# Half-array matmul pairs in two pieces ordered through GpSimd, with new load queues and a new planned order, in a kernel of sliding-window attention and a state-space layer

## The chip, the cores and the metric

The kernel runs on one core of a Trainium2 chip. The metric is the device time of one execution in microseconds (us); lower is better.

## The reference

Two independent layers read inputs of 2048 tokens by 448 features, in bf16, and their results stand side by side in the output (2048 x 896).

```python
# A: attention over 8 keys, 2 tokens apart, 16 heads of 28
qkv = x @ wqkv
logits = einsum("bhsd,bhswd->bhsw", q, k[s - 2*w, w = 0..7]) * 28**-0.5   # masked where s - 2w < 0
a = (softmax(logits) @ v) @ wo
# B: diagonal complex state-space layer with 448 states
Lam_bar = exp(dt * Lam);  B_bar = ((Lam_bar - 1) / Lam)[:, None] * Bmat
h[t] = Lam_bar * h[t-1] + B_bar @ x[t]
y = 2 * real(h @ Cmat.T) + x * Dskip
out = concatenate([a, y], axis=-1)
```

## The kernel before

**Layout.** Two tokens are taken together, so there are 1024 rows of 896 features, which lie across partitions as seven tiles of 128 (`xA`, `xB`, loaded by transposing DMAs). The even token's 448 features are tiles 0 to 2 and the lower half of tile 3, the odd token's the upper half of tile 3 and tiles 4 to 6. A product of both tokens with one weight matrix is therefore made of matmuls with 64 partitions: the lower and the upper half of the TensorE array work side by side, one for each token, and at the fifth pair they change places, so that each writes into the PSUM bank the other wrote into before. That is `pairs` (line 491): four pairs, a `PE.drain()`, three pairs. The weights must lie in both halves of the partitions, so copies on DVE fill the second one: `n_vw` (459) for V, `n_wp` (464) and `n_wo2` (471) for Q and K, which are also padded from 28 to 32 columns a head.

**Work units.** The kernel builds a list of nodes, each with its engine or engines, a cost, dependencies and a rank:

- `v0` to `v8` (596): V for nine blocks of 128 rows, evicted by `ev`; `q{q}{s}{c}` (611): Q (q = 0) and K (q = 1) for four groups of heads s and two chunks c of 512 rows, evicted by `eq`.
- `s{par}{b}` (647): scores of one token of the pair for block b; `x` (648, 649): their exponentials on ACT; `a{b}` (666): probabilities times V; `n{b}` (667): the normalisation on DVE (a reciprocal at 663 and a product at 664); `ot{b}`: a transposing DMA of the result.
- `l1`, `l2`, `wtx` (561 to 563): the state-space input weights, made from parameters and tables (`tr`, `pA` to `p3`, `t0` to `t4`) and transposed by DMA; `b{hf}{k}` (749): input products for half hf of the rows and state tile k (k = 3 is half as big), evicted by `be`.
- For each `b`: `ma`, `ri`, `sc`, `mb`, `ro` on DVE (704 to 748): a rotation, the scan, the rotation back, giving the states h. The scans of half 1 start from the end of half 0.
- `cg`, `ch` (779, 780): output weights C from the transposed C, on ACT and DVE; `g0`, `g1`: products C x B for the odd tokens.
- `y{t}` (845): output of the state-space layer for 128 rows; it needs every `ro` of its half, all C and both g. `w{t}` (861): the attention output projection, by `pairs`. Each is evicted to `ys` and stored from SP.

**Order.** `Plan.run` (64) walks through the nodes with a clock for each engine and always takes the ready node of the lowest rank. Its result is the order in which instructions are written; at run time each engine works strictly in that order and waits where an operand isn't there. Four PSUM units of two banks (pool `mm`) are shared by all products; scores take two at once. Nodes that free a unit get a rank below all others (`node`, 510). `RANK` (27) is an empty table. Outside the plan, ahead of it, stand the loads (281 to 296) and GpSimd's constants (301 to 336: identity, zeros of the padding, masks, ones, and four loads of `Ctn`).

```python
for part in (range(4), range(4, 7)):
    for z, (ps, n, lhs, rhs) in enumerate(jobs):
        if part[0]:
            PE.drain()
        for i in part:
            a, b = (0, 1) if i < 4 else (1, 0)
            x = PE.matmul(ps[:, a, 0:n], lhs(0, lo[i]), rhs(0, lo[i]), ...)
            y = PE.matmul(ps[:, b, 0:n], lhs(64, hi[i]), rhs(64, hi[i]), ...)
```

A last part (from line 894) branches into an exact attention when a sum of exponentials overflowed; it isn't taken with these inputs.

Of the kernel before, what the change touches and what calls it, by code (L numbers as in the profile page):

```python
# [17 lines left out]
HALF = 512  # L18
# [8 lines left out]
RANK = {}  # L27
# [185 lines left out]
def kernel(  # L213
# [66 lines left out]
    xbar_x(xA, xA2, 0, 128)  # L280
    ACT.dma_start(Wv[:, 0:3, :], A_wqkv[0:384, 2 * D:3 * D].rearrange("(k p) n -> p k n", p=128))
    ACT.dma_start(Wv[0:64, 3, :], A_wqkv[384:448, 2 * D:3 * D])
    xbar_x(xA, xA2, 128, 256)
    ACT.dma_start(Wraw[:, 0:3, :], A_wqkv[0:384, 0:2 * D].rearrange("(k p) n -> p k n", p=128))
    ACT.dma_start(Wraw[0:64, 3, :], A_wqkv[384:448, 0:2 * D])
    for i, vec in enumerate((B_Lambda_re, B_Lambda_im, B_log_dt, B_Dskip)):
        G.dma_start(rows[7 * i:7 * i + 7, :], vec.rearrange("(c p) -> c p", p=64))
# [22 lines left out]
    G.memset(m0, 1.0)  # L310
    sel(v16(m1), v16(m0), [[0, 8], [1, 16]], ALU.is_equal, 0.0, 0, -1)
    sel(v8(m2), v8(m0), [[1, 16], [0, 8]], ALU.is_equal, 0.0, 16, -1)
    G.tensor_tensor(msk[0:32, 0, :], m1, m2, ALU.add)
    G.memset(m0, 0.0)
    sel(v16(m1), v16(m0), [[0, 8], [-1, 16]], ALU.is_ge, NEG, 7, 1)
    sel(v16(m2), v16(m0), [[0, 8], [1, 16]], ALU.is_ge, NEG, 0, -1)
    sel(v16(m2), v16(m2), [[0, 8], [1, 16]], ALU.is_ge, 0.0, 8, -1)
    G.tensor_tensor(m1, m1, m2, ALU.add)
    sel(m1, m1, [[0, 128]], ALU.is_ge, 0.0, 15, -1)
    sel(m2, m0, [[1, 128]], ALU.is_ge, NEG, 128, -8)  # L320
    sel(m2, m2, [[-1, 128]], ALU.is_ge, NEG, -114, 8)
    sel(m2, m2, [[0, 128]], ALU.is_ge, 0.0, -16, 1)
    G.tensor_tensor(msk[0:32, 1, :], m1, m2, ALU.add)
    for g in range(1, 4):
        G.tensor_copy(msk[32 * g:32 * g + 32, :, :], msk[0:32, :, :])
    G.memset(Vt[:, :, :, :, 28:29].rearrange("p a b h o -> p (a b h) o"), 1.0)
    for i in range(3):
        G.memset(Pb[i][:, :, :, 112:128], 0.0)
    G.memset(rcs[:], 1.0)
    G.memset(Gm[64:128, 3, :], 0.0)  # L330
    ct_r = B_C_re[:, 384:448].rearrange("(k p) n -> p k n", p=112)
    ct_i = B_C_im[:, 384:448].rearrange("(k p) n -> p k n", p=112)
    G.dma_start(Ctn[:, :, 0:64], ct_r)
    G.dma_start(Ctn[:, :, 64:128], ct_i)
    G.dma_start(Ctn[:, :, 128:192], ct_i)
    G.dma_start(Ctn[:, :, 192:256], ct_r)

    def diag():
        dgE = lazy["dgE"] = t_([128, 4, 128], BF16, "dgE", "rG")
        for k in range(4):  # L340
# [21 lines left out]
    lre, lim, ld = f32[:, 0], f32[:, 1], f32[:, 2]  # L362
# [125 lines left out]
    turn = tc.alloc_semaphore("turn")  # L488
    turns = [0]

    def pairs(jobs):

        lo, hi = (0, 1, 2, 3, 4, 5, 6), (4, 5, 6, 3, 0, 1, 2)
        last = {}
        for part in (range(4), range(4, 7)):
            for z, (ps, n, lhs, rhs) in enumerate(jobs):
                if part[0]:
                    PE.drain()  # L500
# [427 lines left out]
```

## Time and profile before

| | |
|---|---|
| median of 3 runs | 169.62 us (169.33 to 170.07) |
| the profiled execution | 167.73 us |
| its span, first to last instruction | 166.0 us |
| busy in the span: PE / DVE / ACT / GpSimd | 142.3 / 100.1 / 92.6 / 18.9 us |
| mean granted clock of TensorE | 0.925 |

PE is TensorE, whose weight loads (PEld) run beside its matmuls; DVE is VectorE, ACT ScalarE, POOL GpSimd, SP the engine that issues most of the DMAs. A busy PE counts matmuls that lie over each other once; the granted clock is 1.0 at 2.4 GHz and 0.5 at 1.2 GHz. In the chain of waits every piece of time is given to what released the next step, back from the last instruction.

### The profile page before, as it was taken

The numbers are of one execution on the slowest core, as the hardware profiler recorded it, in microseconds if no ns is written. First come the engines' busy times: TensorE is split into PE (matmuls) and PEld (weight loads), VectorE is DVE, ScalarE is ACT, GpSimd is POOL, SyncE is SP. The second block draws the span as 40 slices with busy tenths as digits, with TensorE's granted clock in tenths as the row PEclk, the third lists the DMA queues.
The fourth block names the chain that finished last, engine by engine and source line by source line (L and its number), as shares of the span: only waits on it lengthen the run. The fifth ranks groups of instructions, "written<-read, shape, count | busy, mean of one in ns | idle before, by whom it ended". The sixth has DMA issues, their size and how long they took to land.

```text
span 166.0 us, 3493 instructions
## 1 busy us (share of the span) xinstructions
PE 142.3 (86%) x1424; PEld 66.2 (40%) x1430; DVE 100.1 (60%) x210; ACT 92.6 (56%) x113; POOL 18.9 (11%) x48
## 2 busy tenths in 40 slices
PE   6839799999999999999999865963999999999950
PEld 2213234333344434345455453740353443345530
DVE  0545599679999997989999999999300000000000
ACT  2023897884559896679777497980025325523320
POOL 7989900000000000000000000000000000000000
PEclk9987999999999999999999995555599999999998
DMA  5999998338981020200202020622531331513111
GB/s 128 217 231 228 230 213 153 69 70 155 191 158 32 0 57 4 48 4 0 52 0 48 6 48 18 82 52 48 132 116 55 115 111 56 170 60 111 55 59 61
DMA packets 39924, 15.13 MB, mean 91 GB/s; under 512 B 32928, under 2 KB 39840, under 8 KB 39904
## 3 DMA queue, kind: packets, MB, share of 16 engines
q1 hardware_dynamic: 38688, 13.42, 36.2%
q10 hardware_dynamic: 960, 1.20, 3.2%
q0 software_dynamic: 256, 0.23, 0.7%
q8 instruction: 13, 0.21, 0.5%
q14 instruction: 7, 0.06, 0.1%
HBM read 3.16 MB, written 3.67 MB: 41 GB/s over the span
## 4 chain that ended last, share of the span: by engine, by line
PE 60%; DVE 23%; DMA 5%; issue 4%; ACT 4%; SPq 1%; ACTq 0%; DVEq 0%
PE mm L503 29%; PE mm L697 8%; PE mm L837 7%; PE mm L833 6%; DMA xA<-in_A_x_dram 5%; PE mm L835 4%; DVE O L664 4%; DVE C L774 3%; DVE rs L731 3%; PE mm L657 2%; PE mm L504 2%; DVE ra L710 2%; DVE rb L711 1%; DVE rcs L663 1%; ACT P L645 1%
## 5 line engine op out<-in xcount | busy, mean ns | idle before, releaser
L478 ACT CAST ys<-mm 128x896 bf16<-128x896 f32 x16 | 14.5, 905 | 35.4 <-PE mm L840 29.3
L645 ACT ACTIVATE P<-mm 128x896 bf16<-128x896 f32 (+1 forms) x36 | 31.2, 936 | 2.3 <-PE mm L639 2.3
L503 PE MATMUL mm<-xA,Wpad 64*128 64x512 bf16 x112 | 28.7, 378 | 1.3
L504 PE MATMUL mm<-xA,Wpad 64*128 64x512 bf16 x112 | 28.6, 378 | 1.0 <-DVE Wpad L474 1.0
L697 PE MATMUL mm<-xB,WT 128*128 128x512 bf16 x92 | 22.2, 380 | 0.7 <-ACT u L478 0.3
L503 PE MATMUL mm<-Wv,xA 64*128 64x448 bf16 x63 | 16.0, 378 | 3.7 <-DMA xA<-in_A_x_dram 3.0
L504 PE MATMUL mm<-Wv,xA 64*128 64x448 bf16 x63 | 15.9, 378 | 0.4 <-DVE Wv L462 0.4
L833 PE MATMUL mm<-C,h 128*128 128x448 bf16 x56 | 13.5, 379 | 2.9 <-DVE C L774 2.9
L503 PEld LDWEIGHTS <-Wpad 64*128 64x128 bf16 x112 | 8.7, 94 | 17.5 <-issue 10.0
L697 PEld LDWEIGHTS <-WT 128*128 128x128 bf16 x98 | 9.1, 97 | 11.4 <-issue 1.1
L478 ACT CAST Vt<-mm 128x896 bf16<-128x896 f32 x8 | 7.3, 906 | 11.2 <-PE mm L504 11.0
L503 PE MATMUL mm<-wo,OT 64*128 64x448 bf16 x56 | 12.8, 351 | 0.7
L837 PE MATMUL mm<-C,h 128*128 128x448 bf16 x56 | 13.0, 376 | 0.0
L884 DVE TENSOR_SCALAR flag<-mm 1x1 int32<-1x1 f32 x1 | 0.1, 146 | 21.3 <-PE mm L881 21.3
L504 PE MATMUL mm<-wo,OT 64*128 64x448 bf16 x56 | 12.8, 351 | 0.0
L635 PE MATMUL mm<-msk 32*128 32x448 bf16 (+1 forms) x72 | 9.6, 401 | 3.3 <-DVE O L664 3.1
L657 PE MATMUL mm<-Vt,P 128*128 128x29 bf16 x288 | 9.4, 180 | 2.3 <-ACT P L645 2.3
L503 PEld LDWEIGHTS <-xA 64*128 64x128 bf16 x63 | 5.2, 97 | 13.5 <-issue 6.4
L657 PEld LDWEIGHTS <-P 128*128 128x128 bf16 x288 | 8.5, 99 | 4.5 <-issue 2.1
L664 DVE TENSOR_TENSOR O<-mm,rcs 112x896 bf16<-112x896 f32 (+1 forms) x9 | 9.8, 1092 | 0.3
L478 ACT CAST Kt<-mm 128x1024 bf16<-128x1024 f32 x7 | 7.1, 1012 | 4.6 <-PE mm L504 4.6
L504 PEld LDWEIGHTS <-Wpad 64*128 64x128 bf16 x112 | 8.7, 94 | 1.7 <-DVE Wpad L474 1.5
(171 smaller groups left out, 232.8 us busy)
## 6 DMA issues: line engine op xcount, KB each, us to landing
out_dram<-ys SPq DMA_DIRECT2D x16, 224.0 KB, 2.4
Wraw<-in_A_wqkv_dram ACTq DMA_DIRECT2D x1, 672.0 KB, 7.5
wo<-in_A_wo_dram SPq DMA_DIRECT2D x2, 336.0 KB, 3.4
Wv<-in_A_wqkv_dram ACTq DMA_DIRECT2D x1, 336.0 KB, 3.3
natW<-in_B_B_re_dram SPq DMA_DIRECT2D x1, 336.0 KB, 3.7
natW<-in_B_B_im_dram SPq DMA_DIRECT2D x1, 336.0 KB, 4.5
OT<-O SPq DMA_TRANSPOSE x9, 2.5
Wraw<-in_A_wqkv_dram ACTq DMA_DIRECT2D x1, 112.0 KB, 8.4
```

The costliest lines, as they stand in the source:

```text
L478: ACT.copy(o, i)
L503: x = PE.matmul(ps[:, a, 0:n], lhs(0, lo[i]), rhs(0, lo[i]), start=(i == 0), stop=(i == 6), skip_group_check=True)
L504: y = PE.matmul(ps[:, b, 0:n], lhs(64, hi[i]), rhs(64, hi[i]), start=(i == 0), stop=(i == 6), skip_group_check=True)
L635: PE.matmul(at(g)[:, 0:4 * n].rearrange("p (s q) -> p s q", s=4), msk[32 * g:32 * g + 32, 0, :], msk[32 * g:32 * g + 32, 1:2, c0:c0 + n].t ...
L645: ACT.activation(P[:].rearrange("p s g q -> p g s q")[:, 2 * z:2 * z + 2, :, 0:n], h["s"][z][:, :, 0:4 * n].rearrange("p g (s q) -> p g s ...
L657: PE.matmul(av[:, par, 29 * hd:29 * hd + 29], hb_[par]["P"][:, hd // 4, hd % 4, :], Vt[:, par, b, hd, :], start=True, stop=True)
L664: V.tensor_tensor(O[0:n, :].rearrange("p (a h d) -> p a h d", a=2, h=H), avv[0:n, :, :, 0:DH], rc.unsqueeze(3).to_broadcast((n, 2, H, DH)) ...
L697: PE.matmul(ps[:, i, :], WT[:, j, 128 * m:128 * m + 128], xB[:, j, HALF * hf:HALF * hf + HALF], start=(j == 0), stop=(j == 6))
L731: V.tensor_tensor_scan(h["s"][:, i], p["r2"][:, k:k + 1].to_broadcast((128, HALF)), h["v"][:, i], 0.0 if hf == 0 else ini[:, m:m + 1], ALU ...
L833: PE.matmul(ps[:, 0, 0:D], hb[:, m, lo:lo + 128], lazy["C2"][:, m, :], start=(m == 0), stop=False, skip_group_check=True)
L835: PE.matmul(ps[:, 0, 0:D], xB[:, k, tk], Gm[:, k, :], start=False, stop=(k == 3), skip_group_check=True)
L837: PE.matmul(ps[:, 1, 0:D], hb[:, m, lo + 1:lo + 129], lazy["C1"][:, m, :], start=(m == 0), stop=False, skip_group_check=True)
```

## The change

1. `pairs` becomes `pair`, called twice for a block: first with four pairs, later with three. Between them a node on GpSimd (`relay`) writes one element of `tick` after the last two matmuls of the first piece, and the first matmul of the second piece waits for that write. `PE.drain()` is gone. The planner (`halves`) puts the pieces and the relays into the order like other nodes, the relay with a rank below almost everything.
2. Q and K are made for 256, 256 and 512 rows instead of 512 and 512, which is 24 blocks instead of 16, each waiting for its half of the padded weights. `n_wp` does one half of the columns with all copies into the other partitions (`n_wo2` is gone), and may go to ACT or DVE.
3. Loads: the four parameter rows move from GpSimd's queue to ACT's, in another order; Wraw moves from ACT's to SP's, between the first and the second piece of `xA`.
4. GpSimd's constants, the `Ctn` loads and the two diagonals become nodes of the plan, which other nodes depend on; the planner's GpSimd clock starts at 1.3 instead of 16.0.
5. The ranks are a line each in `RANK` (a base and a step for each kind of node), replacing numbers in the code; DVE's part of the scans (`d0`, `d1`) and their products (`b0`, `b1`) have ranks of their own, and `s` and `a` count down in part, so attention blocks come in the order 1, 0, 8, 7, ... 2. Some costs and arrival times of the planner are other numbers.

```diff
-RANK = {}
+RANK = {"v": (-66.54, 10.223), "q0": (48.53, -16.849), "q1": (28.45, 7.586), "s": (-0.92, -1.464), "a": (-18.79, 2.805), ...}
...
     xbar_x(xA, xA2, 0, 128)
-    ACT.dma_start(Wraw[:, 0:3, :], ...)
-    for i, vec in enumerate((B_Lambda_re, B_Lambda_im, B_log_dt, B_Dskip)):
-        G.dma_start(rows[7 * i:7 * i + 7, :], ...)
+    SP.dma_start(Wraw[:, 0:3, :], ...)
     xbar_x(xA, xA2, 128, 256)
...
-    def n_wp(e, q):
+    def n_wp(e, q, z):
+        o = Wpad[:, :, q, 256 * z:256 * z + 256].rearrange(...)[:, :, :, 0:DH]
...
         f(o[0:64, 3], i[0:64, 3])
+        f(o[64:128, 3], i[0:64, 0])
+        f(o[0:64, 4:7], i[64:128, 0:3])
+        f(o[64:128, 4:7], i[0:64, 1:4])
...
-    def pairs(jobs):
+    def behind(x, y):
+        tc.add_manual_dep(x.ins, y.ins.name, SYNC, reason="row tiles")
+    def pair(h, part, ps, n, lhs, rhs):
...
+        for i in (range(4), range(4, 7))[part]:
+            a, b = (0, 1) if i < 4 else (1, 0)
+            x = PE.matmul(ps[:, a, 0:n], lhs(0, lo[i]), rhs(0, lo[i]), ...)
+            y = PE.matmul(ps[:, b, 0:n], lhs(64, hi[i]), rhs(64, hi[i]), ...)
+            if i == 4:
+                behind(x, h["tick"])
+        if part == 0:
+            h["done"] = (x, y)
+
+    def relay(h):
+        k = h["tick"] = G.memset(tick[:, 0:1], 0.0)
+        behind(k, h["done"][0])
+        behind(k, h["done"][1])
...
+    def halves(name, cost, fn, deps, rank, h, at):
+        x = node(name + "_", {"P": 4 * cost}, lambda e: fn(0), deps, rank, alloc="mm", at=at, mode="h")
+        k = node(name + "k", {"G": 0.12}, lambda e: relay(h), [x], -200)
+        return x, node(name, {"P": 3 * cost}, lambda e: fn(1), [k], -50, mode="h")
...
-    for c in range(2):
+    CH = ((0, 256), (256, 512), (512, 1024))
+    for c, (t0_, t1_) in enumerate(CH):
...
-        n1 = node(f"w{t}", {"P": 1.33}, pe, need + [wl], 62 + 3 * t, alloc="mm", mode="h")
+        n0, n1 = halves(f"w{t}", 0.188, pe, need + [wl], ("w", t), h, 0.0)
...
-    plan.run({"P": 5.6, "A": 4.4, "V": 1.0, "S": 19.0, "G": 16.0})
+    plan.run({"P": 5.7, "A": 4.4, "V": 1.0, "S": 19.5, "G": 1.3})
```

On GpSimd, among its constants at the start, before (`mst` and `msk` are the masks, `Vt` gets its column of ones):

```order
L300 AFFINE_SELECT mst<-mst 32x128 x3
L318 TENSOR_TENSOR mst<-mst 32x128
L300 AFFINE_SELECT mst<-mst 32x128 x4
L323 TENSOR_TENSOR msk<-mst 32x128
L325 COPY msk<-msk 32x256 x3
L326 MEMSET Vt 128x288
L328 MEMSET P_79 128x16x16
```

and now, with a relay's memset of `tick` among them:

```order
L536 MEMSET tick 1x1
L333 TENSOR_TENSOR mst<-mst 32x128
L303 AFFINE_SELECT mst<-mst 32x128 x4
L340 TENSOR_TENSOR msk<-mst 32x128
L536 MEMSET tick 1x1
L344 COPY msk<-msk 32x256 x3
L536 MEMSET tick 1x1
L347 MEMSET Vt 128x288
L536 MEMSET tick 1x1
L351 MEMSET P_79 128x16x16
```

The constants stand in the same sequence; the relays of the first four half-array blocks (two of V, two of K and Q) have come to stand between them.

On ACT, from the late exponentials (`P`) to the output evictions (`ys`), before:

```order
L645 ACTIVATE P_81<-mm 128x2x4x112 x2
L645 ACTIVATE P_79<-mm 128x2x4x112 x2
L645 ACTIVATE P_80<-mm 128x2x4x112 x2
L484 ACTIVATE wtmp<-CT,p_ph 128x448
L645 ACTIVATE P_81<-mm 128x2x4x112 x2
L484 ACTIVATE wtmp<-CT,p_ph 128x448
L478 CAST ys<-mm 128x896 x16
```

and now:

```order
L505 CAST u<-mm 128x512
L698 ACTIVATE P_81<-mm 128x2x4x112 x2
L505 CAST ys<-mm 128x896
L698 ACTIVATE P_80<-mm 128x2x4x112 x2
L505 CAST ys<-mm 128x896
L698 ACTIVATE P_79<-mm 128x2x4x112 x2
L505 CAST ys<-mm 128x896
```

All sixteen output evictions stood behind the last exponential; now nine stand ahead of it, five behind, and two are on DVE. The products `y0` to `y6` and `w` stand on PE between the scores in the same way: y0, scores, y1, scores, attention, y2, scores, y3, scores, attention, w0, w5, scores, w6, w7, attention, scores, y4, scores, y5, attention, y6, w3, w4, w1, w2, y7.

On DVE, from the last scan (`rs`) to the guard (`one`), before (`h` are the states, `C` the output weights, `O` the normalised attention):

```order
L731 SCALAR_TENSOR_TENSOR rs<-p_r_160,ini,rv 128x512
L663 RECIPROCAL rcs<-mm 112x32
L664 TENSOR_TENSOR O<-mm,rcs 112x896
L713 TENSOR_TENSOR ra<-rs,tab 128x512
L714 TENSOR_TENSOR ra<-rs,tab 128x512
L744 TENSOR_TENSOR h_1268<-ra 64x512
L745 TENSOR_TENSOR h_1268<-ra 64x512
L774 SCALAR_TENSOR_TENSOR C_1483<-CT,p_sh,wtmp 128x448 x2
L873 MEMSET one 128x1
```

and now:

```order
L784 SCALAR_TENSOR_TENSOR rs<-p_r_120,ini,rv 128x512
L766 TENSOR_TENSOR ra<-rs,tab 128x512
L767 TENSOR_TENSOR ra<-rs,tab 128x512
L797 TENSOR_TENSOR h_1711<-ra 64x512
L798 TENSOR_TENSOR h_1711<-ra 64x512
L716 RECIPROCAL rcs<-mm 112x32
L717 TENSOR_TENSOR O<-mm,rcs 112x896
L716 RECIPROCAL rcs<-mm 112x32
L717 TENSOR_TENSOR O<-mm,rcs 112x896
L927 MEMSET one 128x1
```

The two C instructions behind the last states have moved ahead of the second half's scans, and two normalisations now come behind the last states.

## Rows read from the trace of the kernel before

**Rows 1.** The page's second part: granted TensorE clock, in tenths, 40 slices of 4.15 us.

```profile
PEclk9987999999999999999999995555599999999998
```

**Rows 2.** Stage windows: stretch, length, busy us (count) of PE PEld DVE ACT POOL, clock, DMA.

```profile
4.10:41.80 37.70, 31.96 (x240) 11.67 (x241) 26.78 (x84) 22.70 (x30) 15.98 (x39) 0.95 0.88 175
41.80:90.00 48.20, 46.56 (x556) 21.71 (x558) 45.67 (x80) 37.05 (x44) 0.00 (x0) 1.00 0.25 49
90.00:115.30 25.30, 17.58 (x343) 11.52 (x342) 24.72 (x41) 17.32 (x23) 0.00 (x0) 0.70 0.22 38
115.30:160.30 45.00, 43.40 (x284) 20.29 (x283) 2.57 (x7) 13.61 (x16) 0.00 (x0) 0.94 0.31 98
```

**Rows 3.** The chain that ended last, in order of time: start, us, what.

```profile
55.30 0.90 PE mm L657 x32
...
80.29 3.13 PE mm L697 x14
...
84.22 0.30 PE mm L635 x4
84.52 0.25 PE mm L639 x16
...
108.30 1.09 DVE O L664
...
115.31 1.28 DVE C L774 x2
116.64 0.53 PE mm L833
...
152.99 1.32 PE mm L833 x7
...
156.59 1.32 PE mm L833 x7
...
160.27 0.91 ACT ys L478
```

**Rows 4.** Timeline of PE, QK and w blocks, lower half of the array: start, us, instruction.

```profile
29.50 0.38 PE L503 MATMUL mm<-xA,Wpad 64*128 64x512 bf16 x1
...
29.97 0.38 PE L503 MATMUL mm<-xA,Wpad 64*128 64x512 bf16 x1
...
140.92 0.35 PE L503 MATMUL mm<-wo,OT 64*128 64x448 bf16 x1
...
141.11 0.35 PE L503 MATMUL mm<-wo,OT 64*128 64x448 bf16 x1
...
141.55 0.36 PE L503 MATMUL mm<-wo,OT 64*128 64x448 bf16 x1
```

**Rows 5.** Timeline of the first 19 us, all engines; in brackets idle time and what ended it.

```profile
0.31 0.10 POOL L912 MEMSET const-float32-0.0<- 128x1 f32 x1 [0.31 <-issue]
...
4.11 1.21 DVE L460 COPY Wv<-Wv 64x448 bf16<-64x448 bf16 x1 [2.84 <-DMA Wv<-in_A_wqkv_dram]
...
9.43 0.63 DVE L468 COPY Wpad<-Wraw 128x1344 bf16<-128x1344 bf16 x1 [3.03 <-DMA Wraw<-in_A_wqkv_dram]
...
10.95 0.36 PE L503 MATMUL mm<-Wv,xA 64*128 64x448 bf16 x1 [2.76 <-DMA xA<-in_A_x_dram]
...
17.98 1.04 POOL L336 DMA_DIRECT2D Ctn<-in_B_C_re_dram  x1
```

**Rows 6.** Groups by line on DVE: count, busy us, mean ns, idle before.

```profile
L480 DVE CAST u<-mm 128x1024 bf16<-128x1024 f32 (+1 forms) x2 | 1.9, 954 | 0.8 <-PE mm L697 0.8
...
L480 DVE CAST Kt<-mm 128x1024 bf16<-128x1024 f32 x1 | 1.2, 1218 | 0.0
...
L480 DVE CAST Vt<-mm 128x896 bf16<-128x896 f32 x1 | 1.1, 1095 | 1.5 <-PE mm L504 1.5
...
L473 DVE COPY Wpad<-Wpad 64x3072 bf16<-64x3072 bf16 x1 | 1.0, 1015 | 0.0
...
L469 DVE COPY Wpad<-Wraw 64x448 bf16<-64x448 bf16 x2 | 0.7, 351 | 0.9 <-DMA Wraw<-in_A_wqkv_dram 0.9
```

More of the change, by code (lines that the diff above doesn't have):

```diff
@@ L309 @@
     v8 = lambda m: m.rearrange("p (a b) -> p a b", b=8)
[L310 to L328, printed above, removed]
@@ L329, with g_eye, g_iota, g_pad @@
-    G.memset(rcs[:], 1.0)
-    G.memset(Gm[64:128, 3, :], 0.0)
+    def g_eye(e):
+        G.memset(eye[:], 1.0)
+        sel(eye[:], eye[:], [[1, 128]], ALU.is_equal, 0.0, 0, -1)
+    def g_iota(e):
+        G.iota(iota, [[1, HALF]], base=1, channel_multiplier=0, allow_small_or_imprecise_dtypes=True)
+    def g_pad(e):
+        G.memset(Wpad[:, :, :, :].rearrange("p k q (h c) -> p (k q h) c", c=32)[:, :, 28:32], 0.0)
+    def g_m1(e):
+        G.memset(m0, 1.0)
+        sel(v16(m1), v16(m0), [[0, 8], [1, 16]], ALU.is_equal, 0.0, 0, -1)
+        sel(v8(m2), v8(m0), [[1, 16], [0, 8]], ALU.is_equal, 0.0, 16, -1)
+        G.tensor_tensor(msk[0:32, 0, :], m1, m2, ALU.add)
@@ L331, with g_m5, g_one, g_zero @@
+    def g_m5(e):
+        for g in range(1, 4):
+            G.tensor_copy(msk[32 * g:32 * g + 32, :, :], msk[0:32, :, :])
+    def g_one(e):
+        G.memset(Vt[:, :, :, :, 28:29].rearrange("p a b h o -> p (a b h) o"), 1.0)
+    def g_zero(e):
+        for i in range(3):
+            G.memset(Pb[i][:, :, :, 112:128], 0.0)
+        G.memset(Gm[64:128, 3, :], 0.0)
+    def g_rcs(e):
+        G.memset(rcs[:], 1.0)
     ct_r = B_C_re[:, 384:448].rearrange("(k p) n -> p k n", p=112)
     ct_i = B_C_im[:, 384:448].rearrange("(k p) n -> p k n", p=112)
-    G.dma_start(Ctn[:, :, 0:64], ct_r)
@@ L784 @@
     gn = []
-    dg = [n for n in plan.nodes if n["name"] == "dia"]
+    dg = [n for n in plan.nodes if n["name"] in ("dgE", "dgO")]
     for z in range(2):
@@ L850, with pe @@
         h = {}
-        def pe(e, tk=tk, h=h):
-            ps = h["ps"] = unit()
+        def pe(part, tk=tk, h=h):
+            if part == 0:
+                h["ps"] = unit()
             o, w = OT(), lazy["wo"]
-            pairs([(ps, D, lambda o_, k: o[o_:o_ + 64, k, tk], lambda o_, k: w[o_:o_ + 64, k, :])])
+            pair(h, part, h["ps"], D, lambda o_, k: o[o_:o_ + 64, k, tk], lambda o_, k: w[o_:o_ + 64, k, :])
         def ev(e, h=h):
```

205 lines of the change are left out of this document (111 added, 94 removed).

## Prediction

> **What bounds the kernel now.** Read the page's slices of the granted clock first: it is full nearly everywhere, but stands at 8 and 7 tenths in slices 3 and 4 and at 5 in slices 25 to 29, where PE was waiting [rows 1]. The stage windows say who is the limit there. From 41.8 to 90 PE and DVE are both full (46.6 and 45.7 of 48.2 us). From 90 to 115.3 DVE has 24.7 of 25.3 us, PE only 17.6, at a mean clock of 0.70. After 115.3 DVE is as good as done (2.6 of 45.0 us) and PE works alone, 43.4 of 45.0 us [rows 2]. The chain shows why the two don't overlap: the last scan's result and the last two C instructions on DVE end at 116.6, and only then can the first output matmul finish; all eight y blocks and all eight w blocks stand behind that, to 160.2, with an eviction and a store of 5.8 us after it [rows 3]. So the tail of 45 us is PE work, part of which could have run while PE waited for DVE.
>
> **The half-array pairs.** A w block starts a pair of matmuls every 0.19 us, but 0.44 us pass from its fourth pair to its fifth (141.11 to 141.55); a QK block, takes 0.215 a pair for its 512 columns (0.19 x 512 / 448), and 0.47 there (29.50 to 29.97) [rows 4]. A drain thus costs 0.25 to 0.26 us, and 9 v, 16 QK and 8 w blocks have one each: 33 x 0.25 = 8.4 us of PE time. After the change a relay on GpSimd stands there (41 of them, as 8 QK blocks are split in two), and the order puts at least three pairs of another block between. The relay is not in this trace. Its parts: a memset of one column 0.10 us [rows 5], a handover like DVE's to PE, 0.05 us (115.31 + 1.28 to 116.64) [rows 3], twice; and the last pair ends 0.16 us after its slot (0.35 long, 0.19 apart [rows 4]). That makes 0.36 us from the end of the slot, against a cover of three pairs, 0.57 us (448 columns), 0.64 (512) or 0.32 to 0.43 (256). So I take 0 for it. Lower bound 0; upper bound the drain's 0.25 us each, if GpSimd takes three times as long as its row.
>
> **QK in 256-token pieces.** The columns are the same: 16 half blocks of 0.75 us for 8 of 1.50. Each matmul now has half the columns, with as many weight loads. The attention rows run 32 matmuls of 29 columns, each with a full weight load, in 0.90 us [rows 3], 28 ns each, far below the 107 ns of a 256-column pair; I take nothing, and at most 0.08 us (the loads as long as a 448-column pair) x 7 pairs for the 5 pieces behind the start of the scans, 2.8 us.
>
> **PE's work in the new order.** Units from rows: b 3.13 (14 matmuls), scores 0.30 + 0.25, attention 0.90, y 3.60 (152.99 to 156.59) [rows 3]; v and w 7 x 0.19 = 1.33, QK 7 x 0.215 = 1.50 [rows 4]; the two g together 4 x 1.32 + 0.3 = 5.6. Before the scans: v 11.2 (less the piece done at 6 us), QK 11 x 0.75 + 4 x 1.50 = 14.3, one small b 1.57, one score 0.55: 27.6 us. From there to y4: six b and a small one 20.4, 16 scores 8.8, 8 attentions 7.2, QK 9.8, g 5.6, **four y 14.4 and four w 5.3**: 71.4. From y4 on: 14.4 + 0.55 + 0.9 + 5.3 = 21.2. In all 120.2 us. Switches between half-array, quarter and full-array work are 47 in both orders, so they change nothing.
>
> **The loads.** PE waited for the second piece of x until 10.95 and DVE for Wraw until 9.43, while the three x pieces and Wraw ran from two queues [rows 5]. Now Wraw stands between the first and second piece of x on SP, and the third piece behind both. I take 10.0 for the second piece (bounds 9 and 12, the latter if Wraw's issue of 1.1 us only pushes it back). The parameter rows move from GpSimd to ACT, which lets GpSimd start its constants earlier. Against this, the four Ctn issues (about 1 us each [rows 5]) now stand between two relays; the cover there is about 2.65 us of PE work, so some 1.2 us show, and some 0.3 at another constant. The lost clock of slices 3 and 4, 0.5 x 4.15 = 2.1 us [rows 1], I leave in, as PE still waits before that load. PE reaches the first big b at 10.0 + 27.6 + 3.9 = 41.5.
>
> **DVE.** Up to the first scan it was busy 26.8 of 37.7 us [rows 2]. Evictions: before 1.22 + 1.10 + 1.22, after five of 1.10, six of 0.69 (1.9 for two, less 1.22) and one of 1.22 [rows 6], +7.3; the Wpad copies go from 10752 columns to 4928, at 1.015 us for 3072 [rows 6], -1.9, the other two nodes being on ACT, which has 15 us free there [rows 2]. That is 32.2. Of 10.9 us idle, 3.0 alone was the wait for Wraw [rows 5], which comes sooner, as do the parameter rows; I keep 4.0 (bounds 2 and 10.9). First scan at 4.1 + 32.2 + 4.0 = 40.3, against 41.8. From there to the last scan's result: busy 70.4 before [rows 2], less two normalisations (1.09 each, the reciprocals left out) that now come later, plus two C instructions (0.64 each) that now come earlier [rows 3], plus 0.7 of evictions: 70.2. With the same 3.1 us idle, 113.6.
>
> **The sum.** Both engines arrive at y4 together: DVE at 113.6, PE at 41.5 + 71.4 = 112.9. Two full engines that feed each other lose something; I add 0.9: 114.5. PE ends at 114.5 + 21.2 + 0.7 = 136.4 (160.2 before), the span at +5.8 = 142.2, the profiled time at +1.7 (167.7 against a span of 166.0) = 143.9, 23.8 less than that execution. The median of the runs, 169.62, stands 1.9 above the profiled one; 169.62 - 23.8 = **146**. The floor is PE without a stall from 9 us: 129.2 at its end, 139 as a median.
>
> **Rivals.**
> 1. *The two engines stall on each other.* Four PSUM units serve scores (two each), y, b and w; a late normalisation on DVE holds the scores, PE waits in order, and the y blocks don't fill the gap. For: from 90 to 115.3 exactly this left PE 69% busy at a clock of 0.70 [rows 2]. Against: no y stood in the order there. At 86% for the 71.4 us, 83 instead of 73: +10, **156** (150 to 160).
> 2. *The relay costs what the drain did*, so the split saves nothing. 17 relays lie behind the start of the scans: +4.3, **150**. Against: its row is 0.10 us.
> 3. *DVE's copies hold GpSimd up.* At the start a DVE copy of 64 x 448 took 1.21 us while GpSimd wrote its constants; later copies of the same size had a mean of 0.35 [rows 5, 6], so the two engines seem to hold each other up. The relays before 40 us run beside the Wpad copies (4928 columns, 1.6 us) and six scalings of the tables and weights. If twice the copies' time shows, PE comes to the scans 3 us later: **149**. [...]
> 4. *Slower than before: the round trip through GpSimd.* PE waits in order, so a late relay holds everything behind it. If a relay takes 1.1 us rather than 0.36, 0.7 us show beyond the cover of most blocks: 41 x 0.7 = 28.7, **175**. It decides from 0.6 us exposed per relay, less if the gaps lower the clock as in slices 25 to 29. Against: nothing in the trace is near that, except GpSimd's own long instructions, and before it had none behind 41.8 us [rows 2].
>
> **How the numbers follow.** Chances: the forecast 0.55 (140 to 150), rival 1 0.21, rival 2 0.12, rival 3 0.08, rival 4 0.04. The range of 139 to 156 takes in the floor and leaves out half of rival 1, rival 4 and a few hundredths below. All but rival 4 are faster by more than 0.5% (0.85 us, about what a measurement of this kernel can tell): 0.95; within it 0.01; slower 0.04.
>
> **What would show it.** Right: y0 to y3 run on PE between the scores, ahead of the last scan's result; that result comes at 111 to 116; PE from then to its last matmul takes some 22 us; PE's clock stays at 10 tenths between 45 us and the end; the fifth pair of a block starts as soon as the other block's pairs are through. Wrong in rival 1's way: PE under 90% between 45 and 115 us, with waits for DVE or ACT. In rival 2's or 4's: PE waiting for GpSimd, 0.25 us or more at each relay. In rival 3's: only before 40 us. The forecast falls altogether if the last scan's result comes later than 120 us.

## The result and the profile after

The changed kernel takes **146.05 us** (median; 145.08 to 146.57 in the compared runs) against 169.48 us in the runs of the kernel before beside it: a ratio of **0.860, 95% interval 0.853 to 0.867**. The median takes in one run of 148.56 us from the chip's slower state; the other three have a median of 145.52. The profiled execution took 145.52 us, its span is 143.8 us, TensorE's mean granted clock 0.974. Busy in the span are PE 130.1, DVE 108.0, ACT 91.7 and GpSimd 21.7 us.

The page's slices of the changed kernel, 3.6 us each, in tenths:

```profile
PE   6949689996999999999999999999999999999920
DVE  0449969995999999999999979999999940343300
PEclk9986999999999999999999999999999999999995
```

Beside [rows 1], the long gap of the clock (at 5 in slices 25 to 29) is gone, and one near the start is left (slices 3 and 4). PE is full from slice 11 on, and DVE, but for a 7 in slice 24, to the end of its scans in slice 32.

Stage windows, cut at the first scan's first product and at the end of the last states (stretch, length, busy us of PE PEld DVE ACT POOL, clock, DMA):

```profile
4.10:44.07 39.97, 34.35 (x370) 18.75 (x371) 31.92 (x94) 28.07 (x42) 16.98 (x55) 0.96 0.94 172
44.07:115.38 71.31, 70.85 (x945) 39.07 (x948) 69.35 (x119) 54.50 (x70) 1.15 (x13) 1.00 0.35 70
115.38:137.40 22.02, 22.02 (x220) 12.02 (x217) 6.22 (x10) 8.23 (x10) 0.35 (x4) 1.00 0.43 114
```

These answer to [rows 2]. The middle stretch has PE at 70.85 and DVE at 69.35 of 71.31 us at full clock. The tail, in which PE works without DVE's scans, has shrunk from 45.0 to 22.0 us. The start is now the loose part: PE waits 5.6 of 40.0 us there and DVE 8.0.

The chain that ended last, in order of time, shows what moved (start, us, what; compare [rows 3]):

```profile
90.04 1.33 PE mm L886 x7
...
103.37 1.43 PE mm L886 x7
...
115.95 1.43 PE mm L886 x7
...
135.86 1.32 PE mm L890 x7
137.47 0.91 ACT ys L505
```

y0 starts at 90.04, y3 at 103.37, the first block that needs the second half's states (y4) at 115.95, 0.57 us after these are there. PE was not waiting for them; it was busy with scores until then (timeline of PE):

```profile
43.80 3.18 PE L750 MATMUL mm<-xB,WT 128*128 128x512 bf16 x13
...
114.48 0.97 PE L710 MATMUL mm<-Vt,P 128*128 128x29 bf16 x32
115.38 0.37 PE L688 MATMUL mm<-msk 32*128 32x448 bf16 x4
115.58 0.37 PE L692 MATMUL mm<-Qt,Kt 28*128 28x112 bf16 x16
115.88 1.31 PE L886 MATMUL mm<-C,h 128*128 128x448 bf16 x6
```

From the first big b at 43.80 on, PE's only wait in its list is one of 0.24 us, so its own work sets the time of y4.

The relay, in the timeline of the w blocks on PE (lower half of the array) and GpSimd, and by its group (start, us, instruction; the group: count, busy us, mean ns):

```profile
128.79 0.35 PE L528 MATMUL mm<-wo,OT 64*128 64x448 bf16 x1
...
129.54 0.35 PE L528 MATMUL mm<-wo,OT 64*128 64x448 bf16 x1
129.73 0.35 PE L528 MATMUL mm<-wo,OT 64*128 64x448 bf16 x1
...
130.30 0.35 PE L528 MATMUL mm<-wo,OT 64*128 64x448 bf16 x1
```

```profile
129.27 0.09 POOL L536 MEMSET tick<- 1x1 f32 x1 [15.64 <-PE mm L529]
130.02 0.09 POOL L536 MEMSET tick<- 1x1 f32 x1 [0.67 <-PE mm L529]
```

```profile
L536 POOL MEMSET tick<- 1x1 f32 x41 | 5.5, 134 | 109.0 <-PE mm L529 108.8
```

The fourth pair of w3 starts at 128.79, four pairs of w4 follow, and w3's fifth comes at 129.73, in the same step of 0.19 us as every other pair; where a drain stood it was 0.44 [rows 4]. The write of `tick` stands at 129.27, well inside; w4's own, with a cover of only three pairs, ends at 130.11, 0.38 us after its last pair's slot and 0.19 ahead of the fifth pair at 130.30. PE's matmuls waited for a relay once in the list of waits, 0.28 us at 27.00, behind one of GpSimd's longer constants; that pair started 0.65 us after the one before instead of 0.19.

### The profile page after: what moved, and what is told of

Its sections match the earlier page's. It is cut to its first block, busy times and chain, and to the rows that moved or that the text cites. A ratio compares the mean times of both kernels' runs of the same rounds, so it can differ in the third digit from the quotient of the medians.

```text
span 143.8 us, 3777 instructions
## 1 busy us (share of the span) xinstructions
PE 130.1 (90%) x1537; PEld 70.9 (49%) x1542; DVE 108.0 (75%) x223; ACT 91.7 (64%) x121; POOL 21.7 (15%) x84
## 4 chain that ended last, share of the span: by engine, by line
PE 77%; DVE 7%; ACT 4%; DMA 4%; POOL 2%; issue 1%; POOLq 0%; ACTq 0%
PE mm L528 24%; PE mm L750 13%; PE mm L886 8%; PE mm L890 7%; PE mm L710 6%; PE mm L888 4%; PE mm L848 4%; DMA WT<-natW 4%; PE mm L946 3%; PE mm L688 3%; PE mm L692 2%; DVE Vt L507 2%; ACT P L698 1%; POOL dgO L303 1%; PE mm L893 1%
## 5 line engine op out<-in xcount | busy, mean ns | idle before, releaser
L528 PE MATMUL mm<-xA,Wpad 64*128 64x256 bf16 (+1 forms) x168 | 27.0, 308 | 1.6 <-DVE Kt L507 1.3
L505 ACT CAST ys<-mm 128x896 bf16<-128x896 f32 x14 | 12.5, 906 | 23.2 <-PE mm L893 19.1
L529 PE MATMUL mm<-xA,Wpad 64*128 64x256 bf16 (+1 forms) x168 | 27.0, 308 | 0.0
L536 POOL MEMSET tick<- 1x1 f32 x41 | 5.5, 134 | 109.0 <-PE mm L529 108.8
L528 PEld LDWEIGHTS <-Wpad 64*128 64x128 bf16 x168 | 15.3, 96 | 10.2 <-issue 0.9
L529 PEld LDWEIGHTS <-Wpad 64*128 64x128 bf16 x168 | 15.1, 96 | 2.2 <-issue 2.2
L528 PE MATMUL mm<-Wv,xA 64*128 64x448 bf16 x63 | 15.1, 380 | 1.1 <-DMA xA<-in_A_x_dram 0.4
L529 PE MATMUL mm<-Wv,xA 64*128 64x448 bf16 x63 | 15.1, 380 | 0.0
L886 PE MATMUL mm<-C,h 128*128 128x448 bf16 x56 | 11.9, 353 | 0.0
L890 PE MATMUL mm<-C,h 128*128 128x448 bf16 x56 | 11.9, 353 | 0.0
L529 PE MATMUL mm<-wo,OT 64*128 64x448 bf16 x56 | 11.2, 350 | 0.0
L528 PE MATMUL mm<-wo,OT 64*128 64x448 bf16 x56 | 11.1, 350 | 0.0
L505 ACT CAST Kt<-mm 128x512 bf16<-128x512 f32 (+1 forms) x9 | 6.6, 728 | 5.2 <-PE mm L529 5.2
L716 DVE RECIPROCAL rcs<-mm 112x32 f32<-112x32 f32 (+1 forms) x9 | 3.1, 344 | 8.3 <-PE mm L710 8.2
L784 DVE TENSOR_TENSOR_SCAN rs<-p_r,ini,rv 128x512 bf16<-128x512 f32 x7 | 8.7, 1272 | 0.0
```

The lines of the kernel that those rows point to most:

```text
L505: ACT.copy(o, i)
L784: V.tensor_tensor_scan(h["s"][:, i], p["r2"][:, k:k + 1].to_broadcast((128, HALF)), h["v"][:, i], 0.0 if hf == 0 else ini[:, m:m + 1], ALU ...
L886: PE.matmul(ps[:, 0, 0:D], hb[:, m, lo:lo + 128], lazy["C2"][:, m, :], start=(m == 0), stop=False, skip_group_check=True)
L890: PE.matmul(ps[:, 1, 0:D], hb[:, m, lo + 1:lo + 129], lazy["C1"][:, m, :], start=(m == 0), stop=False, skip_group_check=True)
```

## Experiments

In every one the rest of the kernel is as changed, unless said; "the reference" is the changed kernel. Its second set of runs, beside experiments 5 to 7:

> The changed kernel itself, as a reference on the same chip for the runs beside it: 145 to 147 by every theory.

Measured: 145.48 us, ratio to before 0.861 (0.855 to 0.866). As expected.

### 1. All y and w blocks planned behind the last states

```diff
-        n1 = node(f"y{t}", {"P": 3.68}, pe, [rout[hf, k] for k in range(4)] + c1 + c2 + gn, ...)
+        n1 = node(f"y{t}", {"P": 3.68}, pe, [rout[1, k] for k in range(4)] + c1 + c2 + gn, ...)
-        n0, n1 = halves(f"w{t}", 0.188, pe, need + [wl], ("w", t), h, 0.0)
+        n0, n1 = halves(f"w{t}", 0.188, pe, need + [wl] + [rout[1, k] for k in range(4)], ("w", t), h, 0.0)
```

> The changed kernel, but every y and w block must wait for the last scan's result, so that all sixteen stand behind it on PE as in the kernel before; everything ahead of y0 stays in the same order. My theory (the new place of four y and four w is the main gain): 4 x 3.60 + 4 x 1.33 = 19.7 us of PE work move behind the last scan's result, while PE has nothing in their place; 146.0 + 19.7 = 166, 163 to 169 with some clock lost, and PE's granted clock falls below 10 tenths between 90 and 115 us. Rival (the split pairs and the loads make most of the gain): 148 to 154.

Measured: 158.64 us (155.85 to 161.24), 157.88 in the profiled execution, 12.4 more than the changed kernel's; the shortest run is 10 above it. The window from 90.0 to 108.3 us, in the changed kernel and in this one:

```profile
90.00:108.30 18.30, 18.30 (x233) 10.61 (x230) 17.99 (x29) 9.68 (x13) 0.00 (x0) 1.00 0.46 102
```

```profile
90.00:108.30 18.30, 10.48 (x267) 7.58 (x257) 17.55 (x31) 12.32 (x15) 0.00 (x0) 0.64 0.54 90
```

PE loses 7.8 us of it to waits, and the mean clock is 0.64, much as [rows 2] had it from 90 us on. So the place of these blocks is about half of the gain, 10 to 12 us and not 19.7. My figure left out two things. Scores and attentions that stood behind y3 were done in the gap instead. And only the planner's order held the blocks back: at run time y0 waits for its own operands alone, so it started at 108.43, where its turn came, and not behind the last states at 119.6. So this run is not quite the one that was meant, and what it gives is a lower bound:

```profile
108.43 2.73 PE mm L886 x7
```

### 2. The order alone, in the kernel before

```diff
-RANK = {}
+RANK = {"cg": (20.5, 0.1), "ch": (20.5, 0.1)}
```

> The kernel before, with one line changed: the C instructions get a rank ahead of the second half's scans, so that the y blocks can stand between the scores. Drains, loads and 512-row QK chunks are as before. My theory: the order alone brings most of the 23.5 us; PE then works between 90 and 115 us, and the time is 152 to 160. What is left to 146 is the 33 drains (8.4 us at most) and the later start of the scans. Rival (the order needs the split pairs and the searched ranks to pay): 165 to 170.

Measured: 157.71 us, ratio 0.933 (0.923 to 0.942), 11.6 us less than before from one line. Its window, beside the third of [rows 2]:

```profile
90.00:115.30 25.30, 24.66 (x295) 12.77 (x294) 24.65 (x42) 13.68 (x16) 0.00 (x0) 1.00 0.21 63
```

PE has 24.7 us of work there instead of 17.6, at full clock, with drains, loads and 512-row chunks as they were. Experiments 1 and 2 measure the order from both ends and agree on 10 to 12 us.

### 3. A drain for each relay, same order

```diff
+            if i == 4:
+                PE.drain()
             x = PE.matmul(ps[:, a, 0:n], ...)
-            if i == 4:
-                behind(x, h["tick"])
...
     def relay(h):
-        k = h["tick"] = G.memset(tick[:, 0:1], 0.0)
-        behind(k, h["done"][0])
-        behind(k, h["done"][1])
+        return
```

> The changed kernel with a drain in place of each of the 41 relays, everything in the same order. My theory (a relay costs nothing, a drain 0.25 us of PE): 17 drains stand behind the start of the scans, 4.3 us; the 24 ahead of it add up to 6.0 us more where PE sets the start of the scans: 150 to 156. Rival (the relay costs what the drain did, or drains lie in PE's waits): 145 to 147.

Measured: 155.51 us, ratio 0.917 (0.907 to 0.926): 9.5 us for 41 drains, 0.23 each, give or take 0.05 by the two intervals. In the timeline of PE two pairs with a drain between them:

```profile
142.88 0.35 PE L530 MATMUL mm<-wo,OT 64*128 64x448 bf16 x1
143.32 0.36 PE L530 MATMUL mm<-wo,OT 64*128 64x448 bf16 x1
```

The step is 0.44 us again, although three or four pairs of another block now stand ahead of it: a drain costs what it did wherever it stands. The first scan starts at 50.06 instead of 44.07 us, 24 x 0.25 = 6.0 for the 24 drains ahead of it. Nearly all of them are on the path, and rival 2 is out. With the order (10 to 12 us) and the loads (2.9, experiment 5) the drains' 9.5 us come to 22 to 25, against 23.4 in all.

### 4. A longer relay

```diff
-        k = h["tick"] = G.memset(tick[:, 0:1], 0.0)
-        behind(k, h["done"][0])
-        behind(k, h["done"][1])
+        for i in range(6):
+            k = h["tick"] = G.memset(tick[:, 0:1], 0.0)
+            if i == 0:
+                behind(k, h["done"][0])
+                behind(k, h["done"][1])
```

> The changed kernel with six writes of one element in each relay instead of one, so that a relay takes some 0.5 to 0.7 us more; same order. My theory (a cover of three pairs, 0.57 to 0.64 us or 0.32 to 0.43 for 256 columns, against a round trip of 0.36): with 0.9 to 1.1 us the round trip sticks out by 0.3 to 0.5 us at most of the 41 relays, 12 to 20 us of PE waiting, of which at least the 17 behind the start of the scans show: 152 to 166, with PE waiting for GpSimd at most relays. Rival (there is far more cover than three pairs, or other waits take it up): under 149.

Measured: 159.37 us, ratio 0.941 (0.930 to 0.953), 13.3 us more. By the list of waits (us in total, times, longest) and the timeline of PE:

```profile
PE mm L528 <- POOL tick L537: 11.4, 19, 1.7
```

```profile
141.69 0.35 PE L528 MATMUL mm<-wo,OT 64*128 64x448 bf16 x1
...
142.29 0.36 PE L528 MATMUL mm<-wo,OT 64*128 64x448 bf16 x1 [0.25 <-POOL tick L537]
```

The pair behind the relay comes 0.60 us after the one ahead of it instead of 0.19: six writes stick out by 0.41 us, with a cover of four pairs. One write had 0.19 us to spare behind three pairs, so the relay is hidden, but not by much. Rival 4 had its mechanism right (41 x 0.41 would be 16.8 us, and 13.3 were lost), but its condition is not met.

### 5. The loads of before

```diff
-    for i, vec in enumerate((B_log_dt, B_Lambda_re, B_Lambda_im, B_Dskip)):
-        ACT.dma_start(rows[7 * i:7 * i + 7, :], ...)
     xbar_x(xA, xA2, 0, 128)
-    SP.dma_start(Wraw[:, 0:3, :], ...)
-    SP.dma_start(Wraw[0:64, 3, :], ...)
     xbar_x(xA, xA2, 128, 256)
+    ACT.dma_start(Wraw[:, 0:3, :], ...)
+    ACT.dma_start(Wraw[0:64, 3, :], ...)
+    for i, vec in enumerate((B_log_dt, B_Lambda_re, B_Lambda_im, B_Dskip)):
+        G.dma_start(rows[7 * i:7 * i + 7, :], ...)
```

> The changed kernel with the loads of before: the parameter rows from GpSimd's queue ahead of its constants, Wraw from ACT's, the first three pieces of x one after another from SP's; everything else as in the changed kernel. My theory (the second piece of x at 10.95 instead of 9.44 us, Wraw at 9.4 instead of 8.2, GpSimd's constants some 4 us later because four issues stand ahead of them): PE starts its work 1 to 3 us later and that shows at the end: 147 to 149. Rival (the first 20 us are bound by DVE and the constants, not by these loads, or the rows come sooner by themselves): 145 to 146.8.

Measured: 148.34 us, ratio 0.878 (0.873 to 0.883), 2.9 us more than the reference. The parameters' transpose on PE, here and in the changed kernel:

```profile
11.54 0.20 PE L399 MATMUL mm<-eye,rows 28*64 28x28 bf16 x1 [4.09 <-DMA rows<-in_B_Dskip_dram]
```

```profile
8.79 0.20 PE L399 MATMUL mm<-eye,rows 28*64 28x28 bf16 x1 [1.54 <-POOL mst L303]
```

(The second wait is put down to a GpSimd instruction that the transpose doesn't need; the reference's own profile has the same wait, until 8.78, ended by the load of the rows.) The size is as expected, the reason only in part. PE stands at the small parameter rows, 2.75 us later, and takes up V right behind them. DVE's copies of the parameters begin at 11.80 instead of 9.04, and the first scaled weight is ready 2.5 to 2.9 us later, at 30.78. But the second piece of x landed no sooner than 11.58 here either (9.4 us from issue to landing), so on PE this run can't tell the two loads apart. In the kernel before, the same transposes stood behind a block of V, at 13.49 us: the 2.9 us are what the new order needs of the loads, not what the loads would have brought alone.

### 6. Q and K in 512-row chunks

```diff
-    CH = ((0, 256), (256, 512), (512, 1024))
+    CH = ((0, 512), (512, 1024))
```

The order was written out: that of the changed kernel, with each pair of 256-row blocks as one block at the place of the first.

> The changed kernel with Q and K in two chunks of 512 rows again: each pair of 256-row blocks becomes one block at the place of the first, and the rest of the order is kept (two half blocks are moved by one place so that every relay keeps a cover). My theory (256-column pairs cost nothing, and what the pieces bring is that work can stand behind the start of the scans): five half blocks, 5 x 0.75 = 3.75 us of PE, and their evictions come ahead of the first big product and the first scan; 148.5 to 151. Rival 1 (the smaller pieces cost PE something, so that 512 rows are better): under 145.5. Rival 2 (the start of the scans is set by DVE's other work, so nothing changes): 145.5 to 147.

Measured: 145.04 us, ratio 0.859 (0.854 to 0.863): the same as the reference. Start of the scans and the stretch to the last states (windows):

```profile
4.10:45.04 40.94, 35.20 (x327) 16.41 (x326) 33.34 (x93) 28.20 (x40) 15.73 (x52) 1.00 0.90 169
45.04:114.63 69.59, 67.62 (x891) 36.35 (x883) 68.12 (x117) 53.14 (x68) 0.71 (x8) 1.00 0.32 70
```

The first scan comes 1.5 us later than the reference's 43.56, and the stretch behind it is 1.7 us shorter; DVE has 1.2 us less to do in it. My theory counted 3.75 us of PE's work and nothing else. In this profile PE's clock stayed full ahead of the scans (1.00 instead of 0.96), which gives 1.6 us of it back, and behind the first scan PE idled 2.0 us instead of 0.5. The 256-row pieces as such neither cost nor bring anything that shows here.

### 7 to 9. Keeping the clock up, and DVE's Wpad copies first

In the changed kernel PE's clock fell to half from 10.0 to 13.3 us, after its waits between 7.3 and 9.4:

```profile
10.00:13.30 3.30, 3.30 (x22) 1.55 (x20) 3.16 (x12) 2.83 (x6) 1.26 (x4) 0.50 1.01 231
```

Nine matmuls without use were put into that wait, once with and once without DVE's copies `wp11` ahead of `pA` (the last two lines).

```diff
+            if b == 0 and part == 0:
+                warm(7)
...
         PE.transpose(tp[64:128, 0:28], rows[:], eye[0:28, 0:28])
+        warm(2)
...
+    wps = unit()
+    def warm(n):
+        for i in range(n):
+            PE.matmul(wps[:, 0, :], zz[:, 0:128], zz[:, 128:640], start=True, stop=True)
...
+        i, j = ([n["name"] for n in order].index(x) for x in ("pA", "wp11"))
+        order.insert(i, order.pop(j))
```

> The changed kernel with two additions: nine matmuls of 512 columns without use (seven after the first piece of v0, two after the parameter transposes) where PE waits between 7.3 and 9.4 us, so that its granted clock needn't fall; and DVE's copies of Wpad, which wait for nothing but Wraw (there at 8.2 us), ahead of its copies of the parameters, which come at 9.04. My theory (PE's work ahead of the scans is on the path; the half clock from 10.0 to 13.3 us costs 1.65 us, DVE's wait 0.8): 143.5 to 145. Rival (the later waits of 1.3 us for a PSUM unit and 1.3 us for transposed weights take it up): 145.5 to 146.5, with the clock full from 7 us on either way.

> The changed kernel with the nine dummy matmuls alone, constants and Wpad copies where they were. My theory: PE reaches the memsets' stretch 1.6 us sooner, but the evictions it waits for on DVE don't come sooner: 144.8 to 145.6. Rival (the earlier Wpad copies were what spoilt the run with both, and the full clock pays by itself): 143.5 to 144.5.

Measured: 145.56 us (0.862, 0.858 to 0.867) with both and 146.10 (0.860, 0.856 to 0.864) with the matmuls alone: nothing gained. The clock's mean from 4.1 to 13 us was 1.00 in both, instead of 0.81 in the reference, but the half clock had only moved: it came from about 17.3 to 20.7 us, when PE had waited for evictions (the window in the first of the two):

```profile
17.70:20.60 2.90, 2.84 (x24) 1.89 (x25) 0.60 (x2) 2.80 (x6) 1.17 (x3) 0.50 1.20 195
```

Up to 45 us the mean is 0.96 in both, as in the reference up to its first scan. So these runs don't show what a full clock would be worth. DVE and GpSimd in the first of the two, by the timeline:

```profile
11.91 0.59 DVE L503 COPY Wpad<-Wraw 64x672 bf16<-64x672 bf16 x1
12.39 0.09 POOL L539 MEMSET tick<- 1x1 f32 x1
12.42 1.35 POOL L349 MEMSET Vt<- 128x288 bf16 x1
12.52 2.30 DVE L504 COPY Wpad<-Wraw 64x672 bf16<-64x672 bf16 x1
```

A copy of a shape that takes 0.4 to 0.6 us elsewhere took 2.30 beside GpSimd's memsets (2.46 in the other run), and PE then waited 1.64 us (2.19) for the eviction queued behind it. The changed kernel has the same at small instructions, at the same memsets, while an eviction from PSUM keeps its time:

```profile
13.53 1.09 DVE L507 CAST Vt<-mm 128x896 bf16<-128x896 f32 x1
...
13.79 1.36 POOL L347 MEMSET Vt<- 128x288 bf16 x1
...
14.78 1.17 POOL L351 MEMSET P<- 128x256 bf16 x3
14.79 1.19 DVE L384 TENSOR_SCALAR p_f<-p_th 128x4 f32<-128x4 f32 x2
...
16.00 0.50 DVE L426 TENSOR_SCALAR p_kM<-p_f 128x4 f32<-128x4 f32 x1
```

That led to the next one. A third run, with both and the edit of experiment 10 together, was expected to free the gain:

> The same, with the dummy matmuls and the earlier Wpad copies of the run before. My theory: the copy that took 2.30 us takes 0.4, so PE's wait of 1.64 us for the eviction behind it goes, and what the dummies give (full clock from 10 to 13 us) reaches the end: 142.5 to 144.3. Rival (DVE's work up to the first scan is the limit and the gain is lost in other waits): 144.8 to 145.8.

Measured: 146.50 us (0.862, 0.857 to 0.868), nothing again. All DVE copies of Wpad were short this time, but PE then waited 3.02 us, until 22.56 us, for the fourth piece of `xA`, which is behind six loads on SP and took SP 5.65 us to issue (4.01 in experiment 10). The clock was low again at the end of that wait and behind it, at a mean of 0.55 from 22.0 to 25.8 us.

### 10. GpSimd's memsets out of DVE's way

The mask's copies one relay later; the zeros of P and Gm and the ones of Vt between the relays from 28 to 33 us.

```diff
+        after("gm4", "q130k")
+        after("one", "q000k")
+        after("zer", "v7k")
+        for y in ("q110k", "v8k", "v8k"):
+            order.insert([n["name"] for n in order].index(y) + 1, next(n for n in order if n["name"] == "zer"))
         for n in order:
             n["fn"](n["by"])
```

(`after(x, y)` puts x behind y; `zer` does one of its four memsets each time.)

> The changed kernel with three of GpSimd's constants later: the copies of the mask one relay later, the zeros of P and Gm and the ones of Vt between the relays from 28 to 33 us instead of 13.4 to 16.1; PE's, DVE's and ACT's orders unchanged. My theory (DVE and GpSimd hold each other up for whole instructions: the run with the dummy matmuls had one DVE copy of Wpad at 2.30 us where its twins took 0.39, beside these very memsets): DVE's five small instructions at 14.9 to 16.1 us take 0.24 + 0.17 us instead of 0.73 + 0.50, PE's wait of 1.29 us for the eviction behind them shrinks by 0.8, and the end comes 0.5 to 1 us sooner: 144.5 to 145.3. Rival (those instructions are slow for another reason, or the time is lost again at the transposed weights): 145.4 to 146, with the small instructions as slow as before.

Measured: **144.26 us** (143.85 to 145.22), ratio 0.851 (0.847 to 0.855): 1.2 us less than the reference's 145.48 (ratio 0.861, 0.855 to 0.866), and with experiment 11 the fastest kernel of this study. The two instructions in it, and a later scaling on DVE:

```profile
14.58 0.24 DVE L396 TENSOR_SCALAR p_f<-p_th 128x4 f32<-128x4 f32 x2
14.78 0.17 DVE L438 TENSOR_SCALAR p_kM<-p_f 128x4 f32<-128x4 f32 x1
...
30.59 2.32 DVE L467 TENSOR_SCALAR tmpB<-tmpB 128x2048 int32<-128x2048 int32 x1
```

The first scan starts at 42.55 us (43.56 in the reference), the last states are done at 113.85 (114.87). Most of this is the theory's: DVE is through these instructions at 14.95 instead of the reference's 16.11 us, 1.16 sooner, of which 0.28 were there before them (the eviction ahead of them starts at 13.31 instead of 13.59) and 0.88 came from the memsets. Two things stand beside it. PE's clock was full from 10 to 13.3 us in this profile, without any dummies:

```profile
10.00:13.30 3.30, 3.01 (x42) 1.78 (x38) 3.14 (x12) 3.25 (x7) 0.88 (x4) 1.00 1.03 243
```

That is not what the gain rests on, as far as the other runs tell: the one with the lowest mean clock, 0.976, took 144.36 us, and a run of the reference at 0.982 took 145.53. And the memsets still collide at their new place, where the scaling of 2048 columns took 2.32 us instead of 1.22 beside the ones of Vt; there no loss shows.

### 11. The fourth piece of x ahead of the loads of B

```diff
     xbar_x(xA, xA2, 256, 512)
+    xbar_x(xA, xA2, 512, 1024)
-    SP.dma_start(natW[:, 0:3, D:2 * D], ...)
-    SP.dma_start(natW[:, 4:7, D:2 * D], ...)
     SP.dma_start(natW[0:64, 3, D:2 * D], ...)
...
     SP.dma_start(Pt[64:128, :], ...)
+    SP.dma_start(natW[:, 0:3, D:2 * D], ...)
+    SP.dma_start(natW[:, 4:7, D:2 * D], ...)
-    xbar_x(xA, xA2, 512, 1024)
```

> The kernel with the later constants, and the fourth piece of xA ahead of the six loads of B on SP's queue, with the two large loads of B last. In the run with the later constants PE waited 1.10 us, and in the one with dummies besides 3.02 us, at the first block of V that needs this piece, which SP issues only from 13.3 to 17.3 us (13.4 to 19.1) behind those six loads. My theory (this load is now the next limit): the piece is there by 18 us, PE's wait of 1.10 us goes, and the time is 142.8 to 143.7. Rival (the loads of B, now issued up to 17 us, make the scaled weights and their transposes late by as much, and PE's wait of 1.02 us for those grows): 144 to 146.

Measured: 144.27 us, the same as experiment 10 (its ratio is 0.846, 0.841 to 0.851; the kernel before took 170.84 us beside it). PE at the small b, in experiment 10 and here:

```profile
32.13 1.68 PE L762 MATMUL mm<-xB,WT 128*128 128x512 bf16 x7 [1.02 <-DMA WT<-natW]
```

```profile
32.04 1.69 PE L762 MATMUL mm<-xB,WT 128*128 128x512 bf16 x7 [1.59 <-DMA WT<-natW]
```

The wait for x is gone, the wait for the transposed weights takes up what it gave. The rival was right in its outcome: the start is bound by the chain from the parameters over the scaled weights to their transposes. Its reason did not come: the second scaled weight was ready at 28.07 instead of 28.74 us, sooner and not later, and the transposes behind it took that much longer. Why they did stays open.

## Why the prediction was right, step by step

The forecast of 146 us met the 146.05 measured, with its mechanism: the order and the relays gave what they were to give. That the number is met to 0.1 us is luck. PE was 3.05 us later at y4 than the sum's path for it; half of that was taken up by two allowances that the sum had put on top for other reasons, and the rest by a smaller step from the profiled execution to the median.

- **The order.** Right: y0 to y3 run between the scores, PE has 70.85 of 71.31 us from the first scan to the last states, the tail is PE at work throughout, with 21.5 us from y4 to its end (21.9 predicted, with 0.7 for which the sum names no row). Experiments 1 and 2 give the order 10 to 12 us.
- **The drains.** Right: 33 x 0.25 = 8.4 us was the estimate; 41 drains put back cost 9.5, and a relay shows only where GpSimd was busy with something longer, at 27.00 us; PE then waited for transposed weights at 33.65 all the same. The 1.2 us for the Ctn issues did not show. My 0.36 us for the round trip against a cover of 0.57 to 0.64 is borne out: the write ends 0.38 us after the slot, and when it is made longer, it shows (experiment 4).
- **The 256-row pieces.** Right as to cost: 256-column pairs start 0.11 us apart, half of 0.215, and experiment 6 finds no difference.
- **The loads.** Mis-sized: I took 0.95 us, for the second piece of x at 10.0 instead of 10.95. PE took it up at 9.44, against 11.70 with the old loads in the new order, and the loads together are worth 2.9 there (experiment 5). The parameter rows, on which DVE and PE's transposes wait, are named in the paragraph on DVE, but have no price in the sum.
- **PE up to the first big b.** The step that failed. The sum has PE there at 41.5 us; it came at 43.80. The work was as counted (15 blocks of Q and K, V, one small b, one score). The 3.9 us of waits were 2.1 for the clock, 1.5 for the relays and 0.3 with no row behind it. The clock cost 1.65 and the relays 0.28; but PE waited 1.28 and 0.67 us for DVE's evictions and 1.28 for the transposed weights, which the sum puts at nothing:

```profile
PE mm L528 <- DVE Kt L507: 1.3, 1, 1.3
PE mm L750 <- DMA WT<-natW: 1.3, 1, 1.3
PE mm L528 <- DVE Vt L507: 0.7, 2, 0.4
```

- **DVE up to the first scan.** The same lateness from DVE's side, and a term that was mis-sized. Its busy time was right, 31.9 us against 32.2. Its idle time, "I keep 4.0 (bounds 2 and 10.9)", was 8.0: 3.08 for the parameters, where it had been 3.03 for Wraw [rows 5], the rest mostly for PE's blocks, which wait in turn for DVE's evictions. First scan at 44.1, not 40.3. The largest of these waits, on DVE in the changed kernel:

```profile
9.04 0.16 DVE L406 CAST p_f<-mm 64x12 f32<-64x12 bf16 x1 [3.08 <-PE mm L400]
```

- **From the first scan to the last states.** 71.3 us on DVE, not 73.3: busy 69.35 (70.2 predicted), and 2.0 instead of 3.1 us idle. But DVE does not set y4: PE took 72.15 us from its first big b to y4 (71.4 predicted) and did not wait for the states, so neither DVE's arrival (113.6 in the sum) nor the 0.9 for mutual stalls lay on the path. They raised PE's 112.9 to 114.5 in the sum, and so hid half of the 3.05 us. y4 came at 115.95, 1.45 later than forecast, and the profiled execution took 145.52, 1.6 more than the 143.9 predicted. The median is as forecast because it stands only 0.5 above the profiled execution, where I had carried over 1.9.
- **Rival 1** (PE and DVE stall on each other) did not come: PE's share between first scan and last states is 99%.
- **Rival 3** is there, smaller and mostly the other way round. A relay in the changed kernel's timeline took 0.97 us beside a DVE scaling of 2048 columns (the next thing PE did was to wait for transposed weights until 33.65, so nothing was lost by it):

```profile
31.88 1.22 DVE L455 TENSOR_SCALAR tmpB<-tmpB 128x2048 int32<-128x2048 int32 x1
32.16 0.97 POOL L536 MEMSET tick<- 1x1 f32 x1 [0.35 <-PE mm L529]
```

  But what cost time were GpSimd's own memsets, beside which DVE's small instructions took 1.19 + 0.50 us (0.73 + 0.50 in the reference's second profile) instead of 0.24 + 0.17. Moving them brought 1.2 us (experiment 10), not the 3 of that rival, and they were not looked at as a cost to DVE. Behind the first scan the relays were free of it, as the rival said: 17 of them took 0.09 us each. The rule of the Trainium skill, SBUF — State Buffer, section "Who interferes with whom", is that between GpSimd and a DVE instruction in a two-port mode whoever comes first locks the other out for the whole instruction. These rows agree with it in kind, in both directions; the copy of 2.30 us was held for longer than one memset. The page also says that a DVE instruction with at most one input from SBUF and outside the two-port modes is left alone; a DVE eviction from PSUM beside the same memset took its usual 1.09 us.

Where PE's order behind the small b, the first product with the transposed weights, is that of the changed kernel, the time from there to y4 is the same whatever happened before: 82.3 us in its two profiles and in experiments 5, 10 and 11, and 82.3 to 82.4 in the three of 7 to 9. It is PE's own work, and the end follows the small b: 2.9 us later in experiment 5 for 2.9 us more time, 1.0 sooner in experiment 10 for 1.2 less. So a gain ahead of it counts as far as it brings the small b forward. The first scan alone doesn't tell this: in experiment 6 it came 1.5 us later, and the time was the same.

What stays open: why SP took 4.01 us to issue the fourth piece of x in experiment 10 and 5.65 in the third run of 7 to 9, and so how much of that run's loss was this one load; and what a full clock in PE's first 20 us would be worth, as no pair of runs differs in that alone.

## What to carry to other kernels

Where the last part of a kernel is one engine working alone, look for the instruction that all of it waits for, and ask which part needs less: here a rank that brings the weights C forward let four of eight output blocks fill another engine's stretch, for 11.6 us and one line. When two engines run full side by side, ask which of the two waits at the handover: here the scores on PE stood in front of y4 while the states were ready. A fixed cost of 0.25 us per block can be hidden behind another block's matmuls through an idle engine, if that engine's own long instructions are kept clear of the handovers. And an idle engine isn't free for its neighbour: before putting GpSimd's constants beside DVE's copies and scalings, look at how long those take there.

## What was not expected of the hardware

- One DVE copy of 64 x 672 bf16 took 2.30 and 2.46 us beside GpSimd's memsets instead of 0.4 to 0.6, longer than the single memset of 1.35 beside it: it seems to have been held over several of them in a row.
- A drain costs the same 0.25 us when other, unrelated pairs stand between it and the pairs it is for.
- Matmuls without use that kept the clock full at 10 us did not remove the half clock: it came back for as long at 17.3 us, after PE's next waits, while in experiments 6 and 10 it stayed away with no such matmuls.
